# The first half of an attention-plus-soft-MoE kernel's stores, moved to the GpSimd queue with one packet per engine

## The chip, the cores and the metric

The kernel runs on one core of a Trainium2 chip. The metric is the device time of one execution in microseconds, the median of several. A profiled execution comes with it: the span runs from the first to the last instruction on the core, and times inside it are counted from its start.

The core has a matrix engine (TensorE, PE in the profile, with PEld for its weight loads), VectorE (DVE), ScalarE (ACT), GpSimd (POOL) and SyncE (SP, which only issues DMAs and waits). Transfers between HBM and the on-chip memory SBUF run on 16 DMA engines. DMAs can be issued from three queues here: GpSimd's (q0, "software_dynamic" in the profile), SyncE's (q1) and ScalarE's (q10, both "hardware_dynamic"). All three feed the same 16 engines.

## What is computed

Sliding-window attention over 8 batches of 8 heads, 576 positions and 64 columns per head; then a soft mixture of experts on the 4608 x 512 result. What matters here is the end:

```python
def _moe_ref(x, phi, w1, w2):
    ...
    d = logits - logits.max(0, keepdims=True)
    d = np.exp(d)
    d /= d.sum(0, keepdims=True) + 1e-09
    slot_input = d.T @ x
    ...
    for e in range(E):
        h = np.maximum(slot_input[e] @ w1[e], 0.0)
        slot_out[e] = h @ w2[e]
    ...
    c = logits - logits.max(1, keepdims=True)
    c = np.exp(c)
    c /= c.sum(1, keepdims=True) + 1e-09
    return (c @ slot_out).astype(np.float32)
```

There are 8 experts with 32 slots in all; `w1` is 8 x 512 x 1024 and `w2` 8 x 1024 x 512, in f32. The output is 4608 tokens by 512 columns in f32, 9.44 MB.

## The kernel before

The attention runs in 8 units (two batches, half of the heads each), software-pipelined over all engines. While they run, GpSimd issues every load: `q`, `k` and `v` of a coming unit, and then expert weights, each converted from f32 to bf16 by the DMA. The loads are issued far ahead, and the queue holds some 20 us of them.

The order of the work is not written by hand. Each operation is declared to a planner (`Prog.op`) with its engine, an estimated cost, a key and what it reads and writes. `Prog.schedule` plays the program through with these estimates and, for each engine, takes the operation that can start first, with the key breaking near ties. GpSimd's and SyncE's operations keep the order of their declaration. `Prog.emit` then writes each engine's list with the semaphore waits that the dependences need.

The last phase, from about 127 us, is the mixture of experts. `slot_input` goes through `w1` (L950) and the second layer `ffn2` (L1011, its matmuls at L1024), which adds up `slot_out` for all 32 slots in one PSUM bank of 512 columns. The last weights to be loaded are those of experts 6 and 7, in column halves: `w26` and `w27` for columns 0 to 255 first, then for columns 256 to 511 (L912 to L915, issued at L481). `ffn2` is therefore run on the first column half up to its end, then `half(0, ...)` (L1064) writes part of the output for those 256 columns, and while it does, the weights of the second column half are still coming in. Then `ffn2` and `half(1, ...)` do the second one.

`half` scales `slot_out` (DVE, L1068) and goes through the first six pairs of 128-token blocks, 256 tokens each. For each pair there is a matmul (L1076 or L1089), a scaling by the token's factor from PSUM to SBUF (L1058 on DVE or L1059 on ACT through `scaled`, L1101 on DVE), and a store:

- pair 0 is stored in two parts of 128 tokens (128 KB each), the first scaled by ACT, the second by DVE;
- pairs 2 and 4 are scaled by DVE in one instruction, pairs 1, 3 and 5 by ACT in two; each is stored in one DMA of 256 KB.

In a half's store each row that lands in HBM is 256 f32 values, 1 KB, and the next row begins 2 KB further. `store` (L1045) declares the DMA (L1053): on SyncE for pairs 0, 2 and 4, on ScalarE for pairs 1, 3 and 5, in both halves. So each half has four stores by SyncE and three by ScalarE, 1.57 MB.

After both halves, the other 24 blocks of 128 tokens are computed over all 512 columns (L1120 to L1144) and stored by SyncE in four DMAs: two of 1 MB, with 8 KB contiguous for each partition, and two of 2 MB, with 16 KB. At the end SyncE waits for every store's semaphore (L1171).

Of the kernel before, what the change touches and what calls it, by code (L numbers as in the profile page):

```python
# [116 lines left out]
class Prog:  # L117
# [6 lines left out]
    def op(self, e, fn, r=(), w=(), a=(), alloc=(), cost=0.5, key=0.0, mode="f",  # L124
           sem=None, nbytes=0, after=(), ndma=1, n=0, port=False):
        o = Op(e, fn, cost, key, mode)
        deps = list(after)
        for b in r:
            deps += b.ready
        for b in w:  # L130
            b.fresh()
            deps += b.prev
        for b in a:
            deps += b.prev
        seen = set()
        for d in deps:
            if d.id not in seen:
                seen.add(d.id)
                o.deps.append(d)
        for b in r:  # L140
            b.reads.append(o)
        for b in list(w) + list(a):
            b.ready.append(o)
        o.wr = [b for b in list(w) + list(a) if b.pool is not None]
        for b in list(r) + list(w) + list(a):
            if b.pool is not None and b not in o.touch:
                b.left += 1
                o.touch.append(b)
        o.alloc = list(alloc)
        o.sems = sem  # L150
        o.bytes = nbytes
        o.ndma = ndma
        o.n = 2 * n
        o.port = port
        self.ops.append(o)
        return o
# [171 lines left out]
def bass_dilated_sliding_attn__then__soft_moe_slots_kernel(  # L328
# [12 lines left out]
    op = P.op  # L341
# [51 lines left out]
    def tile(pool, size=1):  # L393
        t = Buf(pool)
        t.size = size
        return t
# [11 lines left out]
    def bank(t):  # L408
        return ps[:, t.phys[0], :]
# [99 lines left out]
    for i in range(3):  # L509
# [16 lines left out]
       r=[b_id0], w=[b_id], cost=0.3)  # L526
    load_unit(1)

    for y in range(2):
# [3 lines left out]
            r=[b_pre], cost=1.1, key=-1))  # L533
# [3 lines left out]
    def asel(t, sl, base, pat, cm):  # L537
# [7 lines left out]
       r=[b_mask[0]], w=[b_mask[1]], cost=0.6)  # L545
# [16 lines left out]
    for j in range(4):  # L562
# [3 lines left out]
           r=[b_id], w=[b_sel], cost=0.1, key=1)  # L566
        op("dve", lambda g, j=j: g.tensor_copy(fold[32 * j:32 * j + 32, :],
                                               ident[32 * j:32 * j + 32, 32 * j:32 * j + 32]),
           r=[b_id], w=[b_fold], cost=0.1, key=1)
    op("dve", lambda g: g.memset(phi_pad[:], 0.0), w=[b_phi], cost=0.4, key=1)  # L570
    for hi in range(2):
# [3 lines left out]
            r=[b_phist], w=[b_phi], cost=0.2, key=1)  # L575
# [4 lines left out]
       r=[b_phist], w=[b_phi], cost=0.2, key=1)  # L580
# [139 lines left out]
    def st_P(u, g):  # L720
# [12 lines left out]
        def pe(t):  # L733
            for m in range(6):
                i, x = divmod(6 * g + m, 4)
                for half in range(2):
                    o_ = 384 * half + QB * x
                    bk, po_ = (half, m) if ty == 0 else (m // 3, 3 * half + m % 3)
                    i_ = t.matmul(pair(po)[:, bk, 65 * po_:65 * po_ + 65],  # L739
                                  sbt(pts[i])[:, o_:o_ + 128],  # L740
                                  sbt(vn)[:, m, half, 0:65], start=True, stop=True)
            return i_
# [135 lines left out]
    for u in range(NU):  # L878
# [40 lines left out]
       r=[b_csum], w=[b_rcs], cost=0.1, key=K1)  # L919
# [24 lines left out]
    for hh in range(2):  # L944
# [11 lines left out]
        if hh == 0:  # L956
            op("act", lambda ac: ac.activation(h_sb[:, 0:512], pair(hp)[:, 0, :], ACTF.Relu),
               r=[b_hp[0], hp], w=[b_h[0]], cost=0.65, key=K1)
        else:
            op("dve", lambda vv: vv.tensor_scalar(h_sb[:, 512:1024], pair(hp)[:, 1, :], 0.0, None,  # L960
                                                  op0=AluOp.max),
               r=[b_hp[1], hp], w=[b_h[1]], cost=0.65, key=K1)
# [30 lines left out]
    for x in range(2):  # L993
        def rsum(t, x=x):
# [5 lines left out]
           cost=0.8, key=K1 + x, after=[ffn1] if x else [])  # L1000
    op("dve", lambda vv: vv.reciprocal(rtok[:], bank(rs)[:, 0:N_TOK // 128]), r=[rs], w=[b_rtok],
       cost=0.2, key=K1 + 1)
# [39 lines left out]
    def row(d0, n):  # L1042
        return [expT[:, d0 + j:d0 + 128 * n:n] for j in range(n)]

    def store(d0, n, ap, ob, key, h_=None, j=None, e="sp"):  # L1045
        so = DmaSem(nc, f"s_out{d0}_{h_}_{j}")
        s_out.append(so)
        dst = out[d0:d0 + 128 * n, :].rearrange("(p j) f -> p j f", j=n)
        if h_ is not None:
            dst, ap = dst[:, :, CH[h_]], ap[:, :, CH[h_]]  # L1050
        if j is not None:
            dst, ap = dst[:, j], ap[:, j]
        op(e, lambda e: [e.dma_start(dst, ap)], r=[ob], cost=0.5 if e == "act" else 0.1, sem=so,  # L1053
           nbytes=262144 * n // (1 if h_ is None else 2) // (1 if j is None else 2), key=key)

    def scaled(en, d_, s_, k_):
        if en is nc.vector:
            return en.tensor_scalar(d_, s_, k_, None, op0=AluOp.mult)  # L1058
        return en.activation(d_, s_, ACTF.Copy, scale=k_)  # L1059
# [4 lines left out]
    def half(h_, key):  # L1064
        sl = CH[h_]
        mm = []
        e0, e1 = "dve", "act"
        op(e0, lambda en: scaled(en, so_sb[:, sl], bank(sp_)[:, sl], rcs[:, 0:1]),  # L1068
           r=[b_sp[h_], b_rcs, sp_], w=[b_so[h_]], cost=0.45, key=key)
        for o in range(NAB):  # L1070
            d0, ap, prev = AB[o]
            k2 = key + 1 + o
            if o == 0:
                for j in range(2):
                    p1 = tile(psum, 1)
                    mm.append(op("pe", lambda t, j=j, p1=p1: t.matmul(  # L1076
                        bank(p1)[:, 0:256], row(0, 2)[j], so_sb[:, sl], start=True, stop=True),
                        r=[b_so[h_]] + b_expT, w=[p1], alloc=[p1], cost=0.15, key=k2))
                    ob = Buf()
                    op((e1, e0)[j], lambda en, j=j, ap=ap, p1=p1: scaled(  # L1080
                        en, ap[:, j, sl], bank(p1)[:, 0:256], rtok[:, j:j + 1]),
                       r=[p1, b_rtok], a=[ob], after=prev, cost=0.4, key=k2)
                    store(d0, 2, ap, ob, k2, h_, j)
                continue
            p2 = tile(psum, 1)

            def pe(t, d0=d0, p2=p2):
                for j in range(2):
                    i_ = t.matmul(bank(p2)[:, CH[j]], row(d0, 2)[j], so_sb[:, sl],  # L1089
                                  start=j == 0, stop=True, skip_group_check=True)  # L1090
                return i_
            mm.append(op("pe", pe, r=[b_so[h_]] + b_expT, w=[p2], alloc=[p2], cost=0.25, key=k2))
            ob = Buf()
            if o % 2:
                for j in range(2):
                    op("act", lambda en, ap=ap, p2=p2, j=j, o=o: scaled(
                        en, ap[:, j, sl], bank(p2)[:, CH[j]], rtok[:, 2 * o + j:2 * o + j + 1]),
                       r=[p2, b_rtok], a=[ob], after=prev, cost=0.4, key=k2)
            else:
                kr = rtok[:, 2 * o:2 * o + 2].unsqueeze(2).to_broadcast([128, 2, 256])  # L1100
                op("dve", lambda dv, ap=ap, p2=p2, kr=kr: dv.tensor_tensor(  # L1101
                    ap[:, :, sl], bank(p2).rearrange("p (j f) -> p j f", j=2), kr, AluOp.mult),
                   r=[p2, b_rtok], a=[ob], after=prev, cost=0.65, key=k2)
            store(d0, 2, ap, ob, k2 + (0.5 if o % 2 else 0), h_, e="act" if o % 2 else "sp")
        return mm

    ffn2([(e, cc) for cc in range(8) for e in range(4)], None, K1 + 2)
# [3 lines left out]
    ffn2([(7, cc) for cc in range(4)], 0, K1 + 11)  # L1111
    ffn2([(7, cc) for cc in range(4, 8)], 0, K1 + 12)
    mm0 = half(0, K1 + 20)
    ffn2([(6, cc) for cc in range(2, 8)], 1, K1 + 30, after=mm0)
    ffn2([(7, cc) for cc in range(4)], 1, K1 + 31)
# [3 lines left out]
    d0, n0 = 256 * NAB, 2 * NAB  # L1119
    for i, (n, hs) in enumerate(((4, (3,)), (4, (4,)), (8, (5, 6)), (8, (7, 8)))):  # L1120
        if hs[-1] == 8:
            ap = stg[:, 2, 0:8192].bitcast(F32)
        else:
            ap = WD[:, hs[0]:hs[-1] + 1, :].rearrange("p a x -> p (a x)").bitcast(F32)
        ap = ap.rearrange("p (j f) -> p j f", j=n)
        prev = [x for h in hs for x in b_ost[h]]
        ob = Buf()
        for j0 in range(0, n, 2):
            po = tile(psum, 2)

            def pe(t, d0=d0, n=n, j0=j0, po=po):
                for j in range(2):
                    i_ = t.matmul(pair(po)[:, j, :], row(d0, n)[j0 + j], so_sb[:], start=True, stop=True)
                return i_
            key = K1 + 60 + 10 * i + j0
            op("pe", pe, r=b_so + b_expT, w=[po], alloc=[po], cost=0.45,
               key=key)
            for j in range(2):
                op(("act", "dve")[j], lambda en, ap=ap, po=po, j=j, j0=j0, n0=n0: scaled(
                    en, ap[:, j0 + j, :], pair(po)[:, j, :], rtok[:, n0 + j0 + j:n0 + j0 + j + 1]),  # L1140
                   r=[po, b_rtok], a=[ob], after=prev, cost=0.6, key=key)
        store(d0, n, ap, ob, K1 + 70 + 10 * i)
        d0 += 128 * n
        n0 += n  # L1144
# [58 lines left out]
```

## Time and profile before

| | |
|---|---|
| time, median of 3 runs | 175.43 us (175.2 to 175.62) |
| time of the profiled execution | 175.14 us |
| its span | 173.9 us |
| PE / DVE / ACT / POOL busy in the span | 73% / 65% / 55% / 36% |
| q0, GpSimd's queue | 7952 packets, 30.41 MB, 86.9% of 16 engines' span |
| q1, SyncE's queue | 2912 packets, 8.98 MB, 13.3% |
| q10, ScalarE's queue | 1632 packets, 1.57 MB, 2.7% |
| HBM read / written | 61.93 MB / 9.44 MB |
| stores by SyncE of 128 KB / 256 KB | 4 / 4, median 3.0 / 4.1 us from issue to landing |
| stores by ScalarE of 256 KB | 6, median 3.9 us |

Columns of the DMA rows are packets, megabytes and the time that the packets took, as a share of 16 engines over the span or the window shown. Where a packet's record holds both a read and a write that overlap with its neighbours', the shares can add up to more than 100%. Bytes are counted as they are written, so a load that turns f32 into bf16 counts half of what it reads. In the slices of the span, each digit is a share in tenths. A row of the timeline has its start, its length, the engine (with a q for an instruction that only issues a DMA), line, operation and tiles.

### The profile page before, as it was taken

The page shows a single profiled execution, that of the slowest core. Times are in us where ns is not written, and L with a number is a line of the kernel's source. Part 1 is how long each engine was busy: PE and PEld are TensorE (multiplying, and loading weights), DVE is VectorE, ACT ScalarE, POOL GpSimd, SP SyncE. Part 2 cuts the span into 40 slices and gives each one's busy share as a digit, 9 for nine tenths or more (in the row PEclk, how much of TensorE's full clock was granted, in tenths as well). Part 3 has the DMA queues.
Part 4 walks back from the last instruction along what each step waited for, and adds up shares of the span by engine and source line. Part 5 has one row for each costly group of instructions (what it writes and reads, how often), then busy time and mean ns, then how long its engine had stood idle before and what let it go on. Part 6 is the DMA issues. An engine that isn't in the chain of part 4 may idle for free.

```text
span 173.9 us, 5097 instructions
## 1 busy us (share of the span) xinstructions
PE 127.0 (73%) x2235; PEld 97.3 (56%) x2235; DVE 113.8 (65%) x259; ACT 95.9 (55%) x147; POOL 62.8 (36%) x106
## 2 busy tenths in 40 slices
PE   0003778987889999979899799987879896599000
PEld 0003758976678877858787688666553533353000
DVE  6960079769978899886979978999430301489400
ACT  2310791789868878776888587674301101589300
POOL 6950199500996006762001756809700000000000
PEclk9999996999999999999999999999975999969755
DMA  5999999999999999998999999999999999999998
GB/s 170 273 208 197 218 231 196 215 212 214 228 212 207 216 214 209 245 212 189 219 214 216 213 215 220 213 215 219 213 211 209 206 197 196 294 358 396 422 433 351
DMA packets 12517, 41.28 MB, mean 237 GB/s; under 512 B 2128, under 2 KB 8784, under 8 KB 9040
## 3 DMA queue, kind: packets, MB, share of 16 engines
q0 software_dynamic: 7952, 30.41, 86.9%
q1 hardware_dynamic: 2912, 8.98, 13.3%
q10 hardware_dynamic: 1632, 1.57, 2.7%
q8 instruction: 17, 0.28, 0.6%
q14 instruction: 4, 0.03, 0.0%
HBM read 61.93 MB, written 9.44 MB: 410 GB/s over the span
## 4 chain that ended last, share of the span: by engine, by line
PE 35%; DMA 23%; DVE 21%; ACT 7%; POOL 4%; issue 3%
DMA TT<-in_moe_w_dram 15%; DMA stg<-in_v_dram 8%; PE ps L641 7%; PE ps L635 6%; DVE XB L750 6%; PE ps L710 6%; DVE PT L700 4%; PE ps L685 4%; ACT TT L667 3%; PE ps L739 3%; PE ps L794 3%; POOL TT L481 3%; PE ps L767 3%; DVE WD L1058 3%; ACT PT L692 3%
## 5 line engine op out<-in xcount | busy, mean ns | idle before, releaser
L692 ACT ACTIVATE PT<-ps 128x768 bf16<-128x768 f32 x48 | 37.0, 815 | 12.0 <-PE ps L685 11.9
L667 ACT ACTIVATE TT<-ps 128x864 f32<-128x864 f32 x32 | 27.5, 896 | 17.3 <-PE ps L641 11.1
L750 DVE TENSOR_TENSOR XB<-ps,RV 96x768 bf16<-96x768 f32 x32 | 30.1, 945 | 0.5
L641 PE MATMUL ps<-ident,stg 96*128 96x96 bf16 x288 | 15.8, 218 | 16.1 <-DMA stg<-in_v_dram 15.8
L715 DVE COPY VN<-ps 128x768 bf16<-128x768 bf16 x32 | 17.2, 544 | 13.1 <-PE ps L710 12.9
L641 PEld LDWEIGHTS ps<-ident,stg 96*128 96x128 bf16 x288 | 14.4, 105 | 16.9 <-DMA stg<-in_v_dram 15.8
L685 PE MATMUL ps<-TT 64*128 64x96 bf16 x384 | 15.6, 204 | 4.9 <-ACT PT L692 2.3
L739 PE MATMUL ps<-VN,PT 128*128 128x65 bf16 x384 | 17.5, 195 | 2.2 <-issue 1.1
L710 PE MATMUL ps<-ident,TT 128*128 128x128 bf16 x192 | 16.5, 226 | 2.0 <-DVE VN L715 0.8
L608 POOL COPY stg<-stg 96x576 f32<-96x576 f32 x24 | 16.4, 684 | 1.5
L1059 ACT ACTIVATE WD<-ps,rtok 128x256 f32<-128x256 f32 (+1 forms) x22 | 10.5, 553 | 11.6 <-PE ps L1076 10.4
L739 PEld LDWEIGHTS ps<-VN,PT 128*128 128x128 bf16 x384 | 14.7, 99 | 3.2 <-issue 1.1
L685 PEld LDWEIGHTS ps<-TT 64*128 64x128 bf16 x384 | 9.6, 94 | 10.1 <-ACT PT L692 3.9
L710 PEld LDWEIGHTS ps<-ident,TT 128*128 128x128 bf16 x192 | 11.6, 101 | 4.8 <-issue 2.0
L700 DVE TENSOR_TENSOR PT<-PT,mask_d 128x768 bf16<-128x768 bf16 x24 | 14.1, 620 | 0.0
L448 POOL DMA_DIRECT2D stg<-in_q_dram x8 | 4.1, 519 | 26.9 <-PE ps L641 26.9
L767 PE MATMUL ps<-ident,XB 96*128 96x96 bf16 x192 | 11.2, 206 | 1.8 <-DVE XB L750 1.6
L700 DVE TENSOR_TENSOR PT<-PT,mask_p 128x768 bf16<-128x768 bf16 x24 | 12.4, 543 | 0.1
L635 PE MATMUL ps<-ident,stg 96*128 96x96 bf16 x216 | 10.5, 206 | 1.0 <-issue 1.0
L780 ACT ACTIVATE XT<-ps 128x576 bf16<-128x576 bf16 x16 | 9.9, 651 | 1.7 <-PE ps L767 1.7
L767 PEld LDWEIGHTS ps<-ident,XB 96*128 96x128 bf16 x192 | 9.0, 98 | 3.1 <-DVE XB L750 2.6
L635 PEld LDWEIGHTS ps<-ident,stg 96*128 96x128 bf16 x216 | 9.7, 98 | 1.6 <-issue 1.1
(98 smaller groups left out, 206.9 us busy)
## 6 DMA issues: line engine op xcount, KB each, us to landing
WD<-in_moe_w_dram POOLq DMA_DIRECT2D x4, 1024.0 KB, 25.0
stg<-in_moe_w_dram POOLq DMA_DIRECT2D x3, 1024.0 KB, 30.3
stg<-in_q_dram POOLq DMA_DIRECT2D x4, 576.0 KB, 18.0
stg<-in_k_dram POOLq DMA_DIRECT2D x4, 576.0 KB, 20.1
stg<-in_v_dram POOLq DMA_DIRECT2D x4, 576.0 KB, 22.7
stg<-in_q_dram POOLq DMA_DIRECT2D x8, 288.0 KB, 17.4
stg<-in_k_dram POOLq DMA_DIRECT2D x8, 288.0 KB, 19.2
stg<-in_v_dram POOLq DMA_DIRECT2D x8, 288.0 KB, 21.1
```

The costliest lines, as they stand in the source:

```text
L608: return g.tensor_copy(o_, i_)
L635: i_ = t.transpose(bankb2(pt, a)[:, 96 * kk:96 * kk + 96], il_ap(u, j, a)[:, 128 * kk:128 * kk + 128], ident[0:96, 0:96])
L641: i_ = t.transpose(bankb2(pt, a)[:, 96 * kk:96 * kk + 96], two[:, c, :], ident[0:96, 0:96])
L667: return ac.activation(d, sv, ACTF.Copy)
L685: i_ = t.matmul(pair(sc)[:, hx, QB * x:QB * x + QB], win(u, 1, h01, blk_, bpar)[64 * hx:64 * hx + 64], win(u, 0, h01, blk_, bpar)[64 * hx: ...
L692: op("act", lambda ac: ac.activation(sbt(pt)[:, 0:768].rearrange("p (x n) -> p x n", x=2), pair(sc)[:, :, 0:384], ACTF.Exp, scale=SCALE), ...
L700: return dv.tensor_tensor(p_, p_, m.unsqueeze(1).to_broadcast([128, 2, 384]), AluOp.mult)
L710: i_ = t.transpose(bankb(pv)[:, 128 * m:128 * m + 128], win(u, 2, h01, m, bpar), ident[:, :])
L715: op("dve", lambda dv: dv.tensor_copy(sbt(vn)[:, :, :, 0:64], bankb(pv)[:, 0:768].rearrange("p (m x d) -> p m x d", m=6, x=2)), r=[pv], w= ...
L739: i_ = t.matmul(pair(po)[:, bk, 65 * po_:65 * po_ + 65], sbt(pts[i])[:, o_:o_ + 128], sbt(vn)[:, m, half, 0:65], start=True, stop=True)
L750: op("dve", lambda dv: dv.tensor_tensor(sbt(xb)[:].rearrange("p m (x h d) -> p h x m d", x=2, h=2)[:, h01], pv()[:, :, :, 0:64], sbt(rv)[: ...
L767: i_ = t.transpose(bankb(px)[:, QB * m:QB * m + QB], sbt(xb)[:, m, 128 * x:128 * x + 128], ident[0:QB, 0:QB])
```

## The change

Within `half(0, ...)`, every store is now declared on GpSimd, behind the loads in GpSimd's own order. In `half(1, ...)` and after it, everything stays where it was. A DMA that GpSimd issues through `store` has `single_packet=True`: the pieces that one DMA engine gets of it are framed as one packet instead of one packet for each piece. The planner's estimate for a store issued by GpSimd is 0.6 us.

```diff
@@ def store(d0, n, ap, ob, key, h_=None, j=None, e="sp") @@
-        op(e, lambda e: [e.dma_start(dst, ap)], r=[ob], cost=0.5 if e == "act" else 0.1, sem=so,
+        op(e, lambda e: [e.dma_start(dst, ap, single_packet=e is nc.gpsimd)], r=[ob], cost={"act": 0.5, "pool": 0.6}.get(e, 0.1), sem=so,
            nbytes=262144 * n // (1 if h_ is None else 2) // (1 if j is None else 2), key=key)
@@ def half(h_, key) @@
-                    store(d0, 2, ap, ob, k2, h_, j)
+                    store(d0, 2, ap, ob, k2, h_, j, e="sp" if h_ else "pool")
                 continue
...
-            store(d0, 2, ap, ob, k2 + (0.5 if o % 2 else 0), h_, e="act" if o % 2 else "sp")
+            store(d0, 2, ap, ob, k2 + (0.5 if o % 2 else 0), h_,
+                  e=("act" if o % 2 else "sp") if h_ else "pool")
```

In the built program, GpSimd's list ends with seven more DMAs, two of 128 x 256 values and five of 256 x 256; SyncE's list has four fewer and ScalarE's three fewer. What PE and DVE run, and in which order, is the same, and so are ScalarE's activations.

## Prediction

> **What bounds the kernel now.** I read the page's slices first, then the chain, then the DMA queues by window.
>
> ```profile
> DMA  5999999999999999998999999999999999999998
> GB/s 170 273 208 197 218 231 196 215 212 214 228 212 207 216 214 209 245 212 189 219 214 216 213 215 220 213 215 219 213 211 209 206 197 196 294 358 396 422 433 351
> ```
>
> The 16 DMA engines are 90% busy or more in nearly every slice. Loads that turn f32 into bf16 read two bytes for each one counted, so 210 GB/s here is about 420 read. The last slices are stores only. The chain of waits ends on the last scaling, not on the data:
>
> ```profile
> 160.27 2.63 DVE stg L1058 x4
> ```
>
> That scaling is over at 162.9, its store is issued at 162.98, and the issue table gives that store 10.9 us to landing:
>
> ```profile
> out_dram<-stg SPq DMA_DIRECT2D x1, 2048.0 KB, 10.9
> ```
>
> 2.10 MB need only 4.9 us at the rate below. So about 6 us of older stores stood in front: the end is set by how fast the queues drain, and the compute engines have some 6 us to spare. Busy time by window around the hand-over from loads to stores (columns: PE, PEld, DVE, ACT, POOL, clock, DMA share, GB/s):
>
> ```profile
> 146.00:148.00 2.00, 1.24 (x13) 0.96 (x14) 1.00 (x3) 0.62 (x2) 0.00 (x0) 1.00 1.45 196
> 149.00:150.00 1.00, 0.59 (x7) 0.12 (x5) 0.21 (x1) 0.67 (x2) 0.00 (x0) 1.00 1.29 259
> 151.00:153.00 2.00, 1.41 (x14) 1.08 (x11) 1.32 (x3) 0.95 (x3) 0.00 (x0) 0.89 1.06 367
> 153.00:155.00 2.00, 2.00 (x8) 0.91 (x7) 1.36 (x3) 1.47 (x5) 0.00 (x0) 0.50 1.05 360
> 159.00:163.00 4.00, 2.01 (x7) 0.62 (x6) 3.90 (x6) 3.54 (x7) 0.00 (x0) 0.97 1.01 420
> 164.00:173.00 9.00, 0.00 (x0) 0.00 (x0) 0.00 (x0) 0.00 (x0) 0.00 (x0) 0.50 1.01 431
> ```
>
> In none of these windows does the share fall under 1: no gap to close. What can change is the rate. Stores of both column halves go in pieces of 1 KB at about 359 GB/s (151 to 157 us: 2.15 MB), those behind them in pieces of 8 KB and 16 KB at 420 and 431. POOL is idle throughout. The queues from 149.0 to 150.6 us, where loads (q0) and first stores (q1 is SyncE, q10 ScalarE) share the engines (packets, MB, share):
>
> ```profile
> q0 software_dynamic: 266, 0.13, 59.7%
> q1 hardware_dynamic: 252, 0.23, 42.5%
> q10 hardware_dynamic: 109, 0.11, 20.1%
> ```
>
> **The change, part by part.** Seven stores of the first half move: two of 128 KB and two of 256 KB from SyncE, three of 256 KB from ScalarE, 1.573 MB in all. Engine order is otherwise unchanged, PE's and DVE's lists too.
>
> *Loads no longer share.* From 144 to 148 us q0 ran 1572 packets, 393 per us. Its last 266 packets take 266/393 = 0.68 us alone, so loads end at 149.0 + 0.68 = 149.68 instead of about 150.5. The matmuls that wait for the last load (150.84) start some 0.8 earlier, and so does all of the second half. This is off the path; it matters below.
>
> *Cheaper engines.* ScalarE loses three issues of 0.54 to 0.67 us, SyncE four of 0.35 to 0.82. ScalarE's seven scalings (four take 1.57 us, so 0.37 apart) then end at 147.38 + 6 x 0.37 + 0.47 = 150.07, where the last ended at 150.90. Worth nothing in itself: ScalarE then waits for the second half.
>
> *POOL's issues.* POOL takes up no other work there; its last load was issued by 124.95.
>
> ```profile
> 119.73 5.22 POOL L481 DMA_DIRECT2D TT<-in_moe_w_dram  x7
> 147.88 0.83 SPq L1053 DMA_DIRECT2D out_dram<-WD  x2
> 148.61 0.67 ACTq L1053 DMA_DIRECT2D out_dram<-WD  x1
> ```
>
> Its issues of 128, 512 and 768 pieces took 0.55, about 0.78 and 0.86, so 0.63 for 256. Started at about 147.95 (SyncE's first at 147.88), the seven begin at 147.95, 148.50, 149.05, 149.68, 150.31, 150.94, 151.57; their inputs (ScalarE by 150.07, DVE by 149.2) are ready each time. POOL offers 256 KB per 0.63 us, 416 GB/s: just what the engines take, so what it starts late stays late.
>
> *The head.* How long after POOL's issue the first packet runs with an empty queue, no row shows in this stage. SyncE's issue at 147.88 has its first packets between 149.0 and 149.5, about 1.2; POOL's takes 0.2 longer to generate: 1.4 is the near bound. The far one is the kernel's start:
>
> ```profile
> 1.37 0.65 POOL L441 DMA_DIRECT2D stg<-in_q_dram  x1 [0.86 <-POOLq L1188]
> ```
>
> No q0 packet ran before 5.0 us there, and seven had by 5.5: 3.7, but behind SyncE's 1 MB load. I take 1.5, near the stage's own rows. The seven stores can run from 149.45, 150.00, 150.60, 151.23 and so on. Loads cover until 149.68; the two short ones take 0.32 each and end at 150.32; the third is there at 150.60: **an idle gap of about 0.25 us**, and from there supply and demand match. Second-half stores, issued by SyncE from about 151.8 (152.55 less 0.8), reach the engines at 153.0 and cover any later gap. Nothing hides a gap before that. Bounds: 0 (1.2 or less) and 1.97 + 0.5 = 2.5 us (3.7).
>
> *One packet per engine.* Each 256 KB store has 256 pieces, 16 per engine, now framed as one packet. The rows put a fixed cost on each piece: at 16 KB the engines move 431 GB/s, at 1 KB 359. No row has a framed store. Bounds: no effect, 1.573/0.359 = 4.38 us; the rate of 16 KB pieces, 1.573/0.431 = 3.65 us. Between lie the loads of the same queue, which read 1 KB pieces at 2 x 196 = 392 GB/s: 4.01. Framed, these should lie between that and 431: I take 410, **3.84 us, a gain of 0.54**.
>
> The Trainium skill, *DMA: Bandwidth & Descriptors*, section "Why small descriptors are slow", lays about three cycles on every packet on this chip and calls joining worth it only at 256 B or less, so it speaks against this part; by my estimate from its figures (three of 850 MHz, 96 pieces per engine) the gain would be 0.34. The rows above show more per piece, and they decide.
>
> *Sum.* Drain from the end of loads to the last packet, in the profiled execution. Before, by these rates: 149.68 + 4.38 + 4.38 + 2.10/0.420 + 4.19/0.431 = 173.16; the last packets ended about 173.4, so mixing loads and stores cost up to 0.2, which goes as well; I count 0.1. After: -0.54 + 0.25 - 0.10 = **-0.4 us**. That execution took 175.14, of which the span is 173.9; the median shown is 175.43, 0.3 above it. On the median: **175.0 us**.
>
> **Rivals.**
> 1. *Everything good at once:* head at 1.2 and 16 KB rate: -0.73 - 0.2 = 174.5. For it: the descriptors are written while the ring is still running. Against: 1.4 is the near bound.
> 2. *Framing does nothing:* transfers stay at 359. Then -0.1 + 0.25 gives 175.6. For it: if the 359 is the price of writing 1 KB rows at a 2 KB pitch, packets are innocent. Against: q0 already reads 1 KB rows at 2 KB pitch at 392.
> 3. *The engines run dry* (the other side). If POOL's first packet comes 2.5 us after issue, it runs at 150.45: 0.77 idle, then 0.23 and 0.28 before the second and third, 1.28 in all. -0.64 + 1.28 gives +0.64: 176.1. The change turns into a loss where the head passes about 1.9 us. For it: the start's 3.7. Against: there SyncE's pieces stood ahead.
> 4. *DVE holds up POOL's descriptors:* if POOL can't write them while DVE runs 147.92 to 149.21 (two scalings of 0.69), the first store starts from 149.21, its packets at 150.7: 1.0 idle plus 0.5 of pacing, 1.5; -0.64 + 1.5 gives 176.3. Against: between 119.7 and 125 DVE worked too, and no issue passed 0.86. The Trainium skill, *SBUF — State Buffer*, has this as its "DVE blocks DMA" trap for certain DVE modes; no run here shows it so far.
> 5. *It doesn't do what it says:* POOL's list does gain the seven issues, with one wait each, on the scaling alone; nothing is left here but the framing, rival 2.
>
> **How the numbers follow.** Forecast 0.45, its own range 174.6 to 175.4; rival 1 0.07; rival 2 0.20; rival 3 0.20; rival 4 0.08. A measurement of this kernel can tell about 0.2% (0.35 us) from no change, so faster is below 175.08 and slower above 175.78. Faster: 0.36 of the forecast plus 0.07, 0.43. Same: 0.09 + 0.17 + 0.02, 0.28. Slower: 0.03 + 0.18 + 0.08, 0.29. The range runs from rival 1 to rival 3's 176.1 with a little over: 174.5 to 176.2; a head of 3.7 (+1.9, 177.3) stays out.
>
> **What would show it.** Right: q0 carries 1.57 MB more and its stores run from about 149.7 to 153.8; DMA share stays at 1 but for a quarter of a microsecond near 150.4; the rate from 150.7 to 153 is near 410; matmuls after the last load start near 150.1. Wrong: a slice between 149.5 and 151 with a share well under 1 (rivals 3, 4); POOL issues over 0.7 us with DVE busy (4); a rate of 360 (2). If the share stays full, the rate rises and the time does not fall, the drain is not what sets the end, and my reading of the bound is wrong.

## The result, and the profile after

The changed kernel took **176.25 us** (median of 20 runs, 175.93 to 177.26); the kernel before, run beside it, 175.53 us (20 runs, 174.75 to 177.2). The ratio is **1.0046, 95% interval 1.0029 to 1.0064**: slower, by some 0.7 to 0.8 us, where 175.0 (range 174.5 to 176.2) and a small gain had been forecast. The profiled execution after took 175.99 us with a span of 174.7; before it was 175.14 and 173.9.

The page of the changed kernel, slices and queues (packets, MB, share of 16 engines):

```profile
DMA  5999999999999999999999999999999999999997
GB/s 165 288 207 198 213 227 193 224 208 217 229 206 210 222 211 217 227 206 211 214 215 217 214 214 214 221 214 216 216 203 214 203 196 197 278 331 396 437 431 330
...
q0 software_dynamic: 8448, 31.99, 89.0%
q1 hardware_dynamic: 2080, 8.19, 12.1%
q10 hardware_dynamic: 816, 0.79, 1.3%
```

The slices still read 9 nearly everywhere: a slice is 4.4 us long and a share of 0.9 looks full in it. The rates show the place: slices 35 and 36 (from 148.5 us) went from 294 and 358 to 278 and 331. q0 gained 1.58 MB in only 496 packets; of 1 KB pieces that would be over 1500. The changed kernel by windows of 1 us (columns: PE, PEld, DVE, ACT, POOL, clock, DMA share, GB/s):

```profile
148.00:149.00 1.00, 1.00 (x9) 0.52 (x7) 0.97 (x2) 1.00 (x4) 1.00 (x2) 1.00 1.45 196
149.00:150.00 1.00, 0.35 (x5) 0.10 (x4) 0.00 (x0) 0.81 (x3) 1.00 (x3) 1.00 1.22 293
150.00:151.00 1.00, 0.29 (x4) 0.10 (x4) 0.00 (x0) 0.00 (x0) 1.00 (x3) 1.00 0.85 286
151.00:152.00 1.00, 0.45 (x5) 0.41 (x5) 0.50 (x2) 0.13 (x1) 1.00 (x3) 1.00 0.87 303
152.00:153.00 1.00, 1.00 (x11) 0.91 (x9) 1.00 (x2) 1.00 (x4) 0.60 (x1) 1.00 0.83 270
153.00:154.00 1.00, 0.70 (x4) 0.15 (x2) 1.00 (x3) 0.65 (x3) 0.00 (x0) 1.00 0.93 318
154.00:155.00 1.00, 0.95 (x4) 0.15 (x2) 0.94 (x2) 0.73 (x3) 0.00 (x0) 1.00 0.97 324
```

Before, the share was 1.05 or more in every one of these; this is the kernel before at the worst place:

```profile
150.00:151.00 1.00, 0.16 (x4) 0.10 (x4) 0.00 (x0) 0.64 (x2) 0.00 (x0) 1.00 1.09 355
```

Now the share is under 1 from 150 to 155, at 270 to 324 GB/s where the kernel before moved about 360. From 150 to 152 DVE and ACT are nearly idle and POOL is at work all the time: the 16 DMA engines wait for GpSimd's queue. Timelines of POOL, SP and DVE (start, length, engine, line, operation):

```profile
147.91 4.69 POOL L1053 DMA_DIRECT2D out_dram<-WD  x7 [23.00 <-ACT WD L1059]
...
152.38 8.40 SPq L1053 DMA_DIRECT2D out_dram<-WD  x7
162.76 0.33 SPq L1053 DMA_DIRECT2D out_dram<-stg  x1
...
159.67 2.72 DVE L1058 TENSOR_SCALAR stg<-ps,rtok 128x512 f32<-128x512 f32 x4
```

POOL waits once, for the first scaling; after that its seven issues follow each other without a further wait. The last store is issued at 162.76, even 0.2 earlier than before (162.98), and its issue row has 11.9 us to landing instead of 10.9. (What released it was ScalarE's last scaling, which ended at 162.73.) Compute was not what came late; the queue in front of that store drained later. The forms of the issues, with least, median and greatest duration in ns:

```profile
L1053 POOL DMA_DIRECT2D out_dram<-WD x7: 565/867/1317, 147.9 to 151.3; - x7
```

The trace's packet records give the rest. Stores can be told apart by counting records in order of their start (32 for 128 KB, 64 for 256 KB), so where two stores overlap on the engines a "first packet" is approximate:

| store of the changed kernel | issue, start to end | first packet | behind the issue's end | median of one 4 KB record |
|---|---|---|---|---|
| 128 KB | 147.91 to 148.48 | 149.14 | 0.66 us | 172 ns |
| 128 KB | 148.47 to 149.03 | 149.74 | 0.71 | 172 |
| 256 KB | 149.02 to 149.73 | 150.41 | 0.68 | 187 |
| 256 KB | 149.59 to 150.46 | 151.28 | 0.82 | 188 |
| 256 KB | 150.15 to 151.17 | 152.17 | 1.00 | 192 |
| 256 KB | 150.72 to 151.89 | 152.94 | 1.05 | 192 |
| 256 KB | 151.29 to 152.60 | 153.75 | 1.15 | 189 |

The issues start 0.57 us apart, but from the third on each lasts 0.15 longer than the one before, so they **end 0.72 apart**, and the first packets of the last five are 0.84 apart (3.34 us for four): 312 GB/s, where records of 187 ns would allow 350 (16 x 4096 B / 187 ns). The ends are GpSimd's pace. The lengths grow in the same way, from 0.57 to 1.32 us or little more, in e14 and e15 below, whose stores are issued long before the engines reach them; and in e12, whose stores go to another buffer, the last five issues are shown without overlap, 0.72 to 0.74 long and 0.71 to 0.73 apart.

I call *idle* the time by which fewer than 16 packets were in flight, from 149 to 156 us, as a share of 16 engines. It is 0.02 us before and **0.58 us** after: 0.18 ahead of the third store, 0.14 each ahead of the fourth and the fifth, nothing ahead of the sixth, and the rest mostly around the last. Between these stores the engines run dry. GpSimd's pace alone does not explain it: 256 KB in 0.72 us is 364 GB/s, more than the 350 at which these records run. The first packet also came later and later behind the end of its issue, 0.68, 0.82 and 1.00 us for the third to fifth stores, with the engines short of work each time. What takes that time inside GpSimd's queue is not shown.

The last packet ends at 174.35 instead of 173.40, 0.95 later. Of this 0.56 are idle; 0.13 are idle after 172 us, where the engines now finish less evenly (0.24 against 0.11). The rest, by the medians, is slower records: 384 of GpSimd's at 188 ns instead of four 1 KB records of 46 ns each (184) cost 384 x 4 / 16 = 0.10, and 768 of SyncE's second-half records at 48 ns instead of 46 another 0.10. Together 0.89. The first of these two is rough: by the means (188.4 ns against 4 x 46.9) GpSimd's records cost the same engine time as before, but those of the other two queues overlapped each other (a share of 1.05 or more) and GpSimd's hardly did. The first 8 KB store starts at 159.01 instead of 158.34, so most of the loss is complete by then.

### The profile page after: what moved, and what is told of

Read it like the earlier page. It is cut to its first block, busy times and chain, and to the rows that moved or that the text cites. A ratio compares the mean times of both kernels' runs of the same rounds, so it can differ in the third digit from the quotient of the medians.

```text
span 174.7 us, 5097 instructions
## 1 busy us (share of the span) xinstructions
PE 128.4 (73%) x2235; PEld 99.2 (57%) x2235; DVE 114.1 (65%) x259; ACT 95.9 (55%) x147; POOL 68.5 (39%) x113
## 4 chain that ended last, share of the span: by engine, by line
PE 30%; DMA 22%; DVE 19%; ACT 14%; POOL 4%; issue 2%; ACTq 0%
DMA TT<-in_moe_w_dram 15%; DVE XB L750 7%; DMA stg<-in_v_dram 7%; PE ps L635 7%; PE ps L641 7%; DVE PT L700 5%; ACT WD L1059 4%; PE ps L710 4%; ACT PT L692 4%; ACT TT L667 3%; PE ps L685 3%; POOL TT L481 3%; DVE VN L715 3%; PE ps L739 3%; PE ps L767 2%; PE ps L794 2%
## 5 line engine op out<-in xcount | busy, mean ns | idle before, releaser
L667 ACT ACTIVATE TT<-ps 128x864 f32<-128x864 f32 x32 | 27.7, 898 | 18.2 <-PE ps L641 11.9
L641 PE MATMUL ps<-ident,stg 96*128 96x96 bf16 x288 | 16.5, 225 | 15.5 <-DMA stg<-in_v_dram 15.1
L641 PEld LDWEIGHTS ps<-ident,stg 96*128 96x128 bf16 x288 | 15.3, 109 | 16.2 <-DMA stg<-in_v_dram 15.1
L685 PE MATMUL ps<-TT 64*128 64x96 bf16 x384 | 16.3, 213 | 4.1 <-ACT PT L692 1.7
L710 PE MATMUL ps<-ident,TT 128*128 128x128 bf16 x192 | 17.0, 231 | 0.9 <-DVE VN L715 0.5
L608 POOL COPY stg<-stg 96x576 f32<-96x576 f32 x24 | 17.0, 710 | 1.5
L685 PEld LDWEIGHTS ps<-TT 64*128 64x128 bf16 x384 | 10.3, 98 | 9.6 <-ACT PT L692 3.1
L700 DVE TENSOR_TENSOR PT<-PT,mask_d 128x768 bf16<-128x768 bf16 x24 | 14.8, 649 | 0.0
L1053 POOL DMA_DIRECT2D out_dram<-WD x7 | 4.7, 889 | 23.0 <-ACT WD L1059 23.0
L635 PE MATMUL ps<-ident,stg 96*128 96x96 bf16 x216 | 10.6, 208 | 0.0
```

The costliest lines, as they stand in the source:

```text
L635: i_ = t.transpose(bankb2(pt, a)[:, 96 * kk:96 * kk + 96], il_ap(u, j, a)[:, 128 * kk:128 * kk + 128], ident[0:96, 0:96])
L641: i_ = t.transpose(bankb2(pt, a)[:, 96 * kk:96 * kk + 96], two[:, c, :], ident[0:96, 0:96])
L667: return ac.activation(d, sv, ACTF.Copy)
L685: i_ = t.matmul(pair(sc)[:, hx, QB * x:QB * x + QB], win(u, 1, h01, blk_, bpar)[64 * hx:64 * hx + 64], win(u, 0, h01, blk_, bpar)[64 * hx: ...
L700: return dv.tensor_tensor(p_, p_, m.unsqueeze(1).to_broadcast([128, 2, 384]), AluOp.mult)
L710: i_ = t.transpose(bankb(pv)[:, 128 * m:128 * m + 128], win(u, 2, h01, m, bpar), ident[:, :])
```

## Experiments: is it the frames, the queue or the moment?

Each ratio is to the kernel before, with its 95% interval; idle and record medians are from one profiled execution, which for e5 and e16 took 0.5 us more than their median. "-" lines are the kernel named first.

**Frames.** The changed kernel without frames:

```diff
-op(e, lambda e: [e.dma_start(dst, ap, single_packet=e is nc.gpsimd)], ...
+op(e, lambda e: [e.dma_start(dst, ap)], ...
```

> The seven first-half stores stay on GpSimd, without the framing into one packet per engine. Three theories for the changed kernel's loss (+0.7 us) and its dips in DMA concurrency about every 0.9 us from 150 to 154 us. Completion: a store's end (its semaphore write) stalls a queue that is alone, some 0.2 us for each store; the dips stay, time as the changed kernel, ratio to before 1.003 to 1.006. Supply: GpSimd hands over descriptors too late or too slowly; the same dips or deeper, ratio 1.004 to 1.007. Framing: the coarse packet is what costs; the dips go, records are 1 KB at about 46 ns, ratio 0.999 to 1.002.

1.0075 [1.005, 1.0099], idle 0.63, records 186 ns. The packets of this kernel between 151 and 152.5 us:

```profile
DMA packets 131, 0.40 MB, mean 268 GB/s; under 512 B 33, under 2 KB 33, under 8 KB 131
```

33 packets are under 512 B, none lies between that and 2 KB, and the other 98 are 4 KB each. So GpSimd's queue joined four 1 KB pieces into one record without being asked; "one packet for each piece", as the change was described, is not what it writes without frames. The frames are neither the cause of the loss nor of a gain that can be told: this interval and the changed kernel's overlap.

**One queue for all seven.** The kernel before with ScalarE's three first-half stores on SyncE:

```diff
-store(..., h_, e="act" if o % 2 else "sp")
+store(..., h_, e="act" if o % 2 and h_ else "sp")
```

> The seven first-half stores are all issued by SyncE, none by ScalarE or GpSimd; the rest as before. Completion: one queue alone, so dips at each store's end between 150 and 153 us, ratio 1.003 or more. Supply by GpSimd, and framing: GpSimd and packets play no part, DMA share at or over 1 throughout, ratio 0.999 to 1.002.

1.0017 [0.9986, 1.0049], idle 0.02, records 46 ns per KB. Its windows (columns as above):

```profile
150.00:151.00 1.00, 0.29 (x4) 0.10 (x4) 0.00 (x0) 0.00 (x0) 0.00 (x0) 1.00 1.09 362
151.00:152.00 1.00, 0.46 (x5) 0.42 (x6) 0.51 (x2) 0.14 (x1) 0.00 (x0) 1.00 1.06 362
152.00:153.00 1.00, 1.00 (x9) 0.79 (x7) 1.00 (x2) 1.00 (x4) 0.00 (x0) 0.74 1.07 364
```

The share stays above 1. One queue alone does no harm that shows; it is GpSimd's queue that does.

**GpSimd for some of them.** First pairs 0, 2, 4 by GpSimd and 1, 3, 5 by ScalarE; then pairs 0 to 2 as before and 3 to 5 by GpSimd:

```diff
-e=("act" if o % 2 else "sp") if h_ else "pool"
+e="act" if o % 2 else "sp" if h_ else "pool"            # e3
+e="pool" if o > 2 and not h_ else "act" if o % 2 else "sp"   # e8
```

> First-half stores of pairs 0, 2 and 4 by GpSimd with framing, of pairs 1, 3 and 5 by ScalarE as before: two queues at once. Completion: one queue's data covers the other's ends, DMA share at or over 1 from 150 to 154, ratio 0.998 to 1.001. Supply: GpSimd has 4 stores instead of 7, its last is issued by 150.5, so most of the loss is gone as well, ratio 1.000 to 1.002, with a dip left near 150. Framing: the dips stay in part, ratio about 1.002.

> First-half stores of pairs 0, 1 and 2 as before (SyncE, ScalarE, SyncE), of pairs 3, 4 and 5 by GpSimd with framing: older stores cover the time that GpSimd's first descriptors take. Late descriptors: no dips between 149 and 154 us (share at or over 1), ratio 0.999 to 1.002. Something in GpSimd's stores themselves (their end, their packets): dips stay at those three, ratio 1.002 to 1.004.

e3: 1.0046 [1.0023, 1.007], idle 0.43, records 188 ns. This is the loss of the changed kernel, though the supply theory expected most of it to be gone. In its profile ScalarE's first packet ran only at 150.54, when the dips near 149.5 and 150.1 had passed. e8: 1.0023 [0.9997, 1.0049], idle 0.15, records 186. With three GpSimd stores behind others the idle time is a quarter of the changed kernel's, and the loss is no longer told from none. But two small dips stay, near 151.6 and 152.5, where the theory of late descriptors expected none: older stores cover a part only.

**Source.** Could the tiles read matter (columns 0 to 255 of a 512-column tile, just written by ScalarE and DVE)? e6 is the kernel before, e7 the changed one, both with each half's tile contiguous in SBUF. e9 is the changed kernel at its own moments, but reading another tile:

```diff
-AB = [..., "p (j f) -> p j f", j=2), ...]
+AB = [..., "p (h j f) -> p h j f", h=2, j=2), ...]    # e6, e7
+if h_ == 0:                                            # e9
+    ap = expT[:, 0:2048].bitcast(F32).rearrange("p (j f) -> p j f", j=2)[:, :, 0:256]
```

> The kernel before, with the first six pairs' output tiles laid out in SBUF so that a half's two rows of a token pair lie in one piece of 2 KB per partition; stores on SyncE and ScalarE, the same sizes in HBM. Pitch of the source: the 1 KB records get shorter, 40 to 43 ns instead of 46, both halves together 0.4 to 0.9 us, ratio 0.995 to 0.998. Late descriptors (the pitch plays no part): 46 ns as before, ratio 0.999 to 1.001.

> The changed kernel with the same layout, one piece of 2 KB per partition for each store. Pitch of the source: 4 KB records of 160 ns while they run; GpSimd's supply (364 to 416 GB/s) then falls behind 410 and the dips get deeper, so only part is gained, ratio 1.001 to 1.004. Late descriptors: records stay at 187 ns, dips as they were, ratio 1.003 to 1.006.

> The changed kernel's stores at the changed kernel's moments (each still waits for its pair's scaling), but they read the tensor that the early run at a pitch read; the first column half of the first 1536 tokens holds other values. Two theories for records of 187 ns in the changed kernel against 160 ns when queued early. Late descriptors: 187 ns and dips as in the changed kernel, ratio 1.003 to 1.008. Source (reading the output tiles costs it): 160 to 165 ns, the dips deeper, ratio 1.001 to 1.006.

e6: 1.0017 [0.9987, 1.0048], 46 ns per KB, idle 0.02. e7: 1.0077 [1.0049, 1.0104], 188 ns, idle 0.93. e9: 1.0064 [1.0038, 1.009], 187 ns, idle 0.63. Neither the pitch nor the tile plays a part that shows.

**Rows in HBM.** The changed kernel with the first half's stores into a dense buffer of their own:

```diff
+scr = nc.dram_tensor("scr", (8 * 256, 256), F32, kind="Internal").ap()
...
+if h_ == 0:
+    dst = scr[d0:d0 + 256, :].rearrange("(j p) f -> p j f", j=2)
```

> The changed kernel's first-half stores at the same moments, but into a separate buffer in HBM in which the 1 KB rows follow one another without a gap; the first column half of the first 1536 tokens of the output is not written. Two theories for 4 KB records of 187 ns when stores come late. HBM rows (16 engines at the same place of the same store write 1 KB rows at a pitch of 2 KB and hinder each other): 160 to 170 ns, ratio 1.002 to 1.005. Descriptors (the engines wait for what to do next, whatever the rows): 183 to 190 ns and the same dips, ratio 1.003 to 1.008.

1.0051 [1.0021, 1.0081], 187 ns, idle 0.66. Not the rows either.

**The moment.** Seven GpSimd stores of the same size, reading data that are ready long before, so that they queue behind the last loads from about 126 us:

```diff
+if h_ == 0:
+    ob = b_psA                                          # e4
+    ap = psA_sb[:].rearrange("p (j f) -> p j f", j=2)
```

e5 reads `expT` at the pitch of the real tiles, e10 two free weight slots, e11 is e5 without frames.

> The first-half stores are as in the changed kernel (GpSimd, framed, the same seven shapes), but they read another tensor that is ready at 127 us (the slot sums in f32), so all their descriptors are queued some 20 us before the loads end; the first column half of the first 1536 tokens then holds other values. Completion: the dips at each store's end stay, seven of some 0.2 us, ratio 1.001 to 1.004 (only the head's delay is saved). Supply: no dips, the stores run without a gap from the loads' end, ratio 0.996 to 0.999. Framing: dips stay as under completion.

> As the run with early stores, but they read 1 KB pieces at a pitch of 2 KB inside each partition (another tensor, ready before the loads end), as the changed kernel's stores do; the early run read 2 KB in one piece. The first column half of the first 1536 tokens holds other values. Two theories for the 4 KB records of 187 ns in the changed kernel against 160 ns in the early run. Late descriptors: the engines were fed piece by piece; here, with all queued, records take 160 ns, about 410 GB/s from 150.5 to 153 us, ratio 0.998 to 1.002. Pitch of the source: records take 185 ns, 350 to 360 GB/s and no dips, ratio 1.001 to 1.004.

> The early run once more, reading the buffer that the output tiles lie in (two slots of it that hold loaded weights and are written only later), at the same pitch. The first column half of the first 1536 tokens holds other values. Late descriptors: 160 to 165 ns and no dips from 150 to 153 us, as in the other two early runs; ratio 0.997 to 1.002. Source: 185 to 190 ns, about 350 GB/s, ratio 1.001 to 1.005.

> The early run at a pitch, without the framing into one packet per engine. Framing does nothing: the profile's records are 4 KB and 160 to 165 ns as with it, about 410 GB/s, ratio 0.997 to 1.002. Framing is what joins pieces: records of 1 KB at 42 to 46 ns, 350 to 390 GB/s, ratio 1.000 to 1.004.

| | ratio | idle | record |
|---|---|---|---|
| e4 | 1.0004 [0.9986, 1.0022] | 0.48 us | 160.5 ns |
| e5 | 0.9998 [0.9969, 1.0027] | 1.30 | 160.5 |
| e10 | 0.9995 [0.9974, 1.0016] | 0.78 | 160.5 |
| e11 | 1.0000 [0.9970, 1.0031] | 0.22 | 160.5 |

Issued early, a 4 KB record takes 160 ns, framed or not, and there are no dips until the stores are through. And still the time is that of the kernel before. To see what lead is needed, e5 was released later and later, by one more dependence each:

```diff
-ob.ready = [x for t in b_expT for x in t.ready]
+ob.ready = [x for t in b_expT for x in t.ready] + b_hT[0].ready + b_hT[1].ready   # e14
+ob.ready = [x for t in b_expT for x in t.ready] + chain[-3:-2]                    # e15
+ob.ready = [x for t in b_expT for x in t.ready] + chain[-1:]                      # e16
```

> The seven GpSimd stores of e5_early_pitch (framed, reading expT, so other values land in the first 1536 rows' first half), released by the transposed hidden layer at about 138.3 us instead of at 127. They are written by about 143, some 7 to 10 us before the engines reach them. Theory lead (a 4 KB record takes 160 ns if its descriptors were written well before the engines come to it, 187 if they are written while the engines run out): 160 ns, no dips from 150 to 153, time as e5_early_pitch, ratio 1.000. Theory order (only stores that were queued directly behind the loads, with no break in GpSimd's issuing, run at 160): 187 ns, ratio 1.002 to 1.005.

> The same stores, released by the matmuls of expert 6 on the first half, at about 145 us: issues at about 145.1, 145.7, 146.2, ... 148.9, the engines come to the first at about 149.8 and to the last at about 153. Theory lead with 3 us enough: 160 ns, no dips, ratio 1.000. Theory lead with more than 4 us needed: 187 ns, no dips since the ring is ahead, ratio 1.000 to 1.003. Theory order: as the latter.

> The same stores, released by the last matmuls of the first half at about 147.1, 0.8 us before the stores of the changed kernel, and with no wait for a scaling between them: issues at about 147.2, 147.8, ... 150.6. If the dips are a delay of each store that is issued when the ring is nearly empty, they stay from about the fifth store on (a store per 0.7 us or more), records at 187 ns, idle 0.2 to 0.6 us, ratio 1.002 to 1.005. If the dips of the changed kernel came from GpSimd's waits for the scalings between the issues, they are gone, ratio 1.000 to 1.002.

| | first issue | issue start to first packet, seven stores | record, by store | idle | ratio |
|---|---|---|---|---|---|
| e14 | 140.14 | 9.0 to 9.3 us | 159 to 165 ns | 0.59 us | 0.9999 [0.9971, 1.0027] |
| e15 | 144.77 | 4.3 to 4.7 | 159 to 165 | 0.49 | 0.9987 [0.9958, 1.0016] |
| e16 | 147.20 | 1.8 to 2.7 | 159, 159, 159, 172, 182, 186, 185 | 0.71 | 0.9998 [0.9968, 1.0027] |
| changed kernel | 147.91 | 1.2 to 2.5 | 172 to 192 | 0.58 | 1.0046 [1.0029, 1.0064] |

e16 and e15 by windows, e16 first:

```profile
150.00:151.00 1.00, 0.26 (x4) 0.06 (x4) 0.00 (x0) 0.47 (x2) 1.00 (x3) 1.00 1.03 360
151.00:152.00 1.00, 0.29 (x4) 0.10 (x4) 0.39 (x1) 0.00 (x0) 0.90 (x2) 1.00 0.95 340
152.00:153.00 1.00, 0.85 (x5) 0.64 (x6) 0.35 (x2) 0.47 (x1) 0.00 (x0) 0.62 0.97 348
153.00:154.00 1.00, 1.00 (x7) 0.69 (x6) 0.63 (x2) 0.83 (x3) 0.00 (x0) 0.50 0.92 330
154.00:155.00 1.00, 0.84 (x4) 0.60 (x4) 0.84 (x2) 0.76 (x3) 0.00 (x0) 0.50 0.78 262
155.00:156.00 1.00, 0.94 (x3) 0.38 (x3) 0.41 (x2) 0.74 (x3) 0.00 (x0) 0.67 0.70 237
```

```profile
150.00:151.00 1.00, 0.02 (x4) 0.02 (x4) 0.00 (x0) 0.20 (x1) 0.00 (x0) 1.00 1.09 398
151.00:152.00 1.00, 0.41 (x6) 0.21 (x7) 0.48 (x1) 0.00 (x0) 0.00 (x0) 1.00 1.01 406
152.00:153.00 1.00, 1.00 (x11) 0.90 (x10) 0.70 (x2) 0.81 (x3) 0.00 (x0) 1.00 0.99 389
153.00:154.00 1.00, 0.73 (x5) 0.30 (x3) 1.00 (x3) 0.76 (x3) 0.00 (x0) 1.00 0.79 292
154.00:155.00 1.00, 0.92 (x4) 0.29 (x4) 0.94 (x3) 0.84 (x2) 0.00 (x0) 1.00 0.74 252
```

Only the moment differs between e5, e14, e15 and e16; e9, which reads the same tile at the changed kernel's moments, has the loss. With 0.7 us more lead than the changed kernel (e16) the share stays at 0.95 or more from 150 to 153, and the loss is gone from the median; its idle time lies mostly behind 154, where the second half is waited for. e16's stores do not wait for scalings, but that is not what helps: in the changed kernel POOL waits for the first scaling only, and its seven issues take 4.69 us in all, those of e16 4.70. With 3 us more (e15) the rate is about 400 GB/s. But then the share falls to 0.79 and 0.74 from 153 to 155, with GpSimd long done. The hole has moved: the first half is through, and the second half is not yet there. ScalarE's and SyncE's work for it in e15:

```profile
152.19 1.57 ACT L1065 ACTIVATE WD<-ps,rtok 128x256 f32<-128x256 f32 x4 [1.99 <-PE ps L1082]
...
152.69 8.14 SPq L1059 DMA_DIRECT2D out_dram<-WD  x7
```

The second half's first packet ran at 153.56. e15's faster records save 384 x (184 - 160) ns / 16 = 0.58 us; the hole costs 0.47 (0.49 against 0.02). What is left, 0.1 us, can't be told from nothing, and its interval says the same. The hole was largest in e5, 1.30 us, where the last load ended at 151.12, and smallest in e11, 0.22, where it ended at 150.08; e11's last packet ended at 172.97, 0.43 before that of the kernel before. No run moved the second half, so that the hole is what takes the gain is read from the traces and not shown by an experiment. Nor is it known whether early stores hold up the loads: these ended at 150.08 to 151.12 in the runs issued early (e4, e5, e10, e11, e14, e15), at 150.34 to 150.62 in the kernel before, e2 and e6.

**Fewer, larger stores.** The changed kernel with four tokens per partition, so that the first half is stored in three DMAs of 512 KB, each with 512 pieces of 1 KB; the second half's stores keep their size:

```diff
-GRP = [2] * NAB + [4, 4, 8, 8]
+GRP = [4] * (NAB // 2) + [4, 4, 8, 8]
...
+elif o % 2:
+    store(d0, 4, osts[o // 2]..., obs, k2 + 0.5, h_, e="pool")
```

> The changed kernel with four tokens per partition in the first 1536 tokens, so that GpSimd stores the first half in three DMAs of 512 KB instead of seven; each waits for two pairs, so the first is issued at about 148.6 us instead of 147.9. Two theories for the dips. A delay at each store (it reaches the engines about 1 us after its issue and nothing else is queued): at most two dips after the first store, idle time of the engines from 149 us on 0.3 to 0.5 us instead of 0.6, ratio 1.001 to 1.004. Rate of the descriptors (GpSimd writes them at less than the engines take): the idle time stays at 0.6 us or more, ratio 1.004 to 1.008.

1.0036 [1.0007, 1.0064], idle 0.83, records 189 ns. Windows:

```profile
149.00:150.00 1.00, 0.82 (x10) 0.37 (x7) 0.49 (x1) 1.00 (x4) 0.84 (x2) 1.00 0.77 103
150.00:151.00 1.00, 0.05 (x4) 0.00 (x0) 0.00 (x0) 0.32 (x1) 1.00 (x2) 1.00 0.69 212
151.00:152.00 1.00, 0.30 (x5) 0.12 (x6) 0.48 (x1) 0.00 (x0) 0.37 (x1) 1.00 1.02 332
152.00:153.00 1.00, 1.00 (x10) 1.00 (x10) 0.56 (x2) 0.67 (x2) 0.00 (x0) 1.00 0.88 307
```

POOL's timeline of it:

```profile
149.15 2.22 POOL L1057 DMA_DIRECT2D out_dram<-WD  x3 [25.13 <-DVE WD L1111]
```

Three issues in 2.22 us, 0.73 to 0.76 each, though each has twice the pieces: GpSimd's pace, 0.72 for 256 pieces, is here nearly a price per DMA, not per piece. The first store can only be issued when two pairs are scaled, 1.24 us later, and the engines run short at the head (shares of 0.77 and 0.69) until its first packet at 150.46, 1.3 us behind the issue; behind it there is one dip, near 152, instead of three. This fits a supply that comes by stores, but it does not settle the two theories: the idle time is what the second expected, the ratio what the first did, and the dip near 152 lies 1.4 us after the second issue had ended (150.64). The run does not win, since the head eats what the larger stores save.

No version tried here was faster than the kernel before by an interval that leaves out 1.

## Why the prediction was wrong

**The bound: right.** The end is set by the draining of the queues. The last store was issued 0.2 us earlier than before and landed later; PE, DVE and ACT kept their spare time, and ScalarE's scalings of the first half ended at 149.8 where 150.07 was worked out. Freeing ScalarE and SyncE was worth nothing, as said.

**"Loads end at ... 149.68": wrong.** They ended at 150.25, only 0.2 earlier than before (150.48). Taken away were the stores that shared the engines, but the engines do not finish their parts of the loads together: of the last load's end markers on the 16 engines twelve lie between 149.07 and 149.44, before the forecast moment, and four between 149.80 and 150.26. The matmuls that wait for the last load:

```profile
149.28 0.29 PE L1024 MATMUL ps<-TT,hTT 128*32 128x256 bf16 x4 [0.22 <-DMA TT<-in_moe_w_dram]
150.66 0.29 PE L1024 MATMUL ps<-TT,hTT 128*32 128x256 bf16 x4 [1.09 <-DMA TT<-in_moe_w_dram]
```

They started at 150.66, not "near 150.1" (150.84 before). So the second half came 0.2 us earlier, not 0.8: SyncE issued it from 152.38, and its first packet ran at 153.93, not at the 153.0 that was to cover "any later gap". A cover at 153.0 would have hidden the last dip of the changed kernel, not those at 150 to 152; in e15 it is the hole.

**The head: right in size.** 1.5 us from issue to first packet was taken, 1.23 was measured. The Trainium skill, *DMA: Bandwidth & Descriptors*, section "Latency and other measured facts", gives about 1 us for the first byte on GpSimd's path; the measured 1.23 is a little more.

**"From there supply and demand match" (idle 0.25): a step that failed, by 0.31 us.** The gap of 0.25 forecast ahead of the third store was there, 0.18. What failed is the rest: one head of 1.5 us for every store, and 0.63 us of POOL per 256 KB, 416 GB/s. The ends of the issues are 0.72 apart, and the time from issue to first packet grew from 1.23 us for the first store to 2.01 for the fifth, ahead of which the engines stood short of work. So dips came ahead of the fourth, the fifth and the last store too, and 0.56 us more idle time than before in all. The Trainium skill, *Perfetto Trace Analysis*, section "DMA Instruction — SWDGE (GPSIMD)", has the profiler close such an instruction when the last descriptor has been generated and not when data have moved: here every first packet came 0.66 to 1.15 us behind that mark.

**"I take 410, 3.84 us, a gain of 0.54": the step that failed by most, 0.64 us.** Frames changed nothing that can be told in either place where they were taken away (e1 beside the changed kernel, e11 beside e5), since this queue forms 4 KB records by itself. The 410 GB/s exist, but they belong to the early issue: e15 has 398 to 406, framed; e11 had 423 and 406, unframed. In the changed kernel the records took 187 ns, 350 GB/s, which is the 359 of the 1 KB hardware records or a little less. The gain of 0.54 came out as a loss of 0.10.

**Rivals.** Rival 2 (framing does nothing) was right in that part. Rival 3 (the engines run dry) names what happened, and its 176.1 is close to the 176.25. That closeness is in part luck: it put 1.28 us of idle time into one late head of 2.5 us and kept the faster records, and the head was 1.23, the idle time 0.58, most of it behind the head, and the records no faster. Rival 4 (DVE holds POOL) is not seen: the issues that passed 0.7 us lie from 149.0 on, and from 149 to 151 DVE did not run at all.

So of the forecast of -0.4, -0.54 +0.25 -0.10, the profile after has: +0.10 for the records (by medians), +0.56 for the gaps, and +0.13 and +0.10 for engines that finish less evenly and for SyncE's slower records, neither of which was in the sum. The -0.10 for loads and stores that no longer mix does not show by itself.

**What stays open.** Why a record of a late store takes 187 ns and one of an early store 160 is not settled. Source, pitch, frames and the rows in HBM are excluded by runs; 4.3 us from issue to first packet is enough (e15), 2.3 to 2.7 in e16's last three stores is not, and e13's last store, with 3.1, had 190. Lead alone is not the whole of it: e16's first three stores had only 1.8 to 2.0 us and ran at 159, directly behind the loads.

## What to carry to other kernels

Here, stores that GpSimd issued just in time offered their data 0.7 to 1.2 us after the issue's end and one 256 KB store per 0.8 us, and with nothing else queued the engines ran dry. Compare the pitch of the issue *ends* and of the first packets with the time of one transfer, not the pitch of the starts. Give such a queue some 4 us from issue to first packet (4.3 was enough in e15, 3.1 not in e13), or leave it to loads that are issued far ahead. And before a drain is made faster, look whether the data behind it will be there: a faster first half only reached the hole before the second.

## What the runs showed of the hardware

- GpSimd's queue wrote 1 KB pieces as 4 KB records, with frames and without (e1, e11); SyncE and ScalarE wrote them as 1 KB records of 46 ns. Records of 8 KB took 312 ns and of 16 KB 614, so the 1 KB records have some 8 ns apiece that do not scale (46 - 614/16 = 7.6). A 4 KB record of 160 ns has about the same (160 - 614/4 = 6.5).
- The same 4 KB record took 160 ns (410 GB/s on 16 engines) or 187 (350): 160 where its store was issued over 4 us ahead, or stood directly behind the loads (e16's first three); 172 to 192 where it was issued just in time.
- Back-to-back GpSimd issues of 256 KB start 0.57 us apart, and each shows 0.15 us longer than the last, up to 1.32, whether the engines are behind or idle; they end 0.72 apart. A 512 KB one took 0.73 to 0.76.
- The 16 engines ended the same stream of loads 1.2 us apart (149.07 to 150.26, after).
